# LayerNorm statistics from accumulated sums, and a sync queue that keeps program order for longer

## The chip, the cores and the metric

The kernel runs on one core of one Trainium2 chip, in one launch. The metric is the device time in microseconds (us), lower is better. Beside the time of a run there is one profiled execution, whose trace gives every instruction, its engine, its start and duration, and what ended the wait before it. The engines are PE (matrix multiply, with PEld for its weight loads), DVE (vector), ACT (activation), POOL (GpSimd) and SP, the sync queue, which issues all of this kernel's transfers.

## The reference, cut to what matters

Two residual blocks follow each other on 2048 tokens of width 640: attention with 32 heads over a sliding window of 256, and a gated MLP whose gate mixes tokens. All is fp32.

```python
h  = x + attention(layernorm(x), wqkv) @ wo
n  = layernorm(h)                              # over the 640 columns, eps 1e-5
z  = gelu(n @ w_in)                            # 1728 columns
z1, z2 = z[:, :864], layernorm(z[:, 864:])     # over 864 columns
g  = w_sp @ z2 + b_sp[:, None]                 # w_sp is 2048 x 2048: tokens by tokens
h2 = h + (z1 * g) @ w_out
```

## The kernel before, in words

Tokens go in 16 tiles of 128. Every fp32 product is made of three reduced-precision products: an operand is split in a high part (a copy on ACT) and a low part (raw minus high, on DVE). Many products also use Strassen's scheme, seven block products for eight, whose sums of blocks are DVE work. After attention the kernel goes through these stages:

- **Output projection and first LayerNorm** (loop over `i`, lines 1450 to 1488). In turn `i` PE multiplies tile `i` with `wo` (`proj_o`, 30 matmuls of 320 columns into one of two PSUM accumulators, `acc_tile`), DVE adds the residual to the tile before it (`add_h`, line 1438), and DVE and POOL make its statistics (`bn_h`): two `bn_stats`, one `bn_aggr` and one small addition on DVE (lines 1444, 90, 91), a power and a product on POOL (lines 92, 93). ACT then normalises (`scale_h`, line 97), PE transposes tile `i - 3` (`turn_h`, 5 transposes, line 932), ACT copies the transpose out and SP stores it to `hn_d`. DVE and ACT meanwhile scale and split later attention tiles (`norm_o` line 181, `split_o` lines 189 and 190) and prepare the first half of `w_in` (line 809 and 815, tiles `wraw`, `zl`). SP loads the attention output (`m`), the residual input (`xh`, 5 buffers) and `w_in`.
- **z1** (`z_pair`, steps 0 to 63): eight pairs of tiles, eight steps each; matmuls in line 992, into banks that ACT and DVE empty (lines 815, 809).
- **z2, first half** (`z2_pair` 8 to 11, steps 64 to 79): 15 matmuls a step (line 1050), a gelu out of PSUM on ACT (line 1055), LayerNorm statistics by `bn_stats` (line 1073), normalisation (line 97), and `right_blocks`, which makes the Strassen pieces `ze` and `zl`.
- **First gate** (`first_gate`, steps 80 to 135): eight pairs of seven steps, 12 matmuls a step (line 1160), for the first half of the token sum; the left pieces come from `w_sp` (`fx<-wsp_in`, line 1112), the result goes to `g_d` (lines 1199, 1200).
- **z2, second half** (`z2_pair` 12 to 15, steps 136 to 151) with inputs in buffers of its own (`z_r`, `z_a`), then the **second gate** (steps 152 to 207) and the **output product** (`out_pair`, steps 208 to 263).

Steps run in number order; `at(n, f)` places preparations, loads and stores ahead of step `n`. What order the instructions then stand in is set twice. Inside `manual_schedule` an engine keeps the order in which the code records. Outside it a scheduler orders each engine's instructions by its own timing estimate, and it may put instructions recorded outside a manual stretch ahead of ones recorded inside it. Before, the four engines PE, DVE, ACT and SP are manual from the start to step 62 and again from three steps into the second gate (step 155) to step 201, where the second gate's last pair begins; `ms.close()` and `in_order()` at the end of the code set this. On the chip each engine, SP too, takes its instructions strictly in the order so fixed.

## Time and profile before

| what | value |
|---|---|
| runs | 1110.23, 1115.27, 1112.72 us; median 1112.72 |
| the profiled execution's own time | 1112.77 us |
| its span, first to last instruction | 1111.1 us |
| busy shares of the span | PE 97%, PEld 88%, DVE 72%, ACT 53%, POOL 29% |
| mean granted PE clock | 0.997 |

The profiled execution's own time is 1.7 us over its span and within 0.1 us of the median. A busy PE in this trace need not be a PE at its full pace, as matmuls overlap: the number of matmuls in a stretch says more than its busy time, so the windows view is read with its counts.

### The profile page before, as it was taken

To read this page: it belongs to the slowest core of one execution; us is meant where nothing else is said; L and a number is where in the kernel's file an instruction comes from. 1 tells how busy PE (TensorE), PEld (TensorE's weight loads), DVE (VectorE), ACT (ScalarE), POOL (GpSimd) and SP (SyncE) were. 2 spreads that over 40 slices of the span, in tenths; PEclk is the share of its full clock that TensorE was granted. 3 is DMA by queue.
4 is the path that set the end of the run, shared out by engine and by line. 5 is a ranking of instruction groups with operands and counts; after the bars stand their busy time and mean duration, and the time that the engine had idled before them with its cause. 6 is when DMAs were issued, how large, how long until landed. Compare 5 with 4: busy or idle time off the path is not lost.

```text
span 1111.1 us, 28813 instructions
## 1 busy us (share of the span) xinstructions
PE 1078.4 (97%) x11083; PEld 973.7 (88%) x11083; DVE 804.5 (72%) x2185; ACT 584.8 (53%) x1202; POOL 318.3 (29%) x447
## 2 busy tenths in 40 slices
PE   8999999999999999999999999999999999999998
PEld 8998887668878787689889999999999899998998
DVE  6643444789999898687877678665448899987784
ACT  4443443259988898735565657443336533333331
POOL 4324446777766666723200002000001000000000
PEclk9999999999999999999999999999999999999999
DMA  7833557545565555689565531233431366674542
GB/s 250 295 114 118 175 182 266 174 159 190 187 188 187 175 181 159 186 248 307 210 226 179 200 117 58 78 106 116 140 123 42 119 236 239 242 270 142 192 142 95
DMA packets 92282, 194.74 MB, mean 175 GB/s; under 512 B 11952, under 2 KB 46272, under 8 KB 88256
## 3 DMA queue, kind: packets, MB, share of 16 engines
q1 hardware_dynamic: 92144, 192.90, 53.0%
q8 instruction: 87, 1.43, 0.5%
q14 instruction: 51, 0.42, 0.1%
HBM read 127.90 MB, written 64.95 MB: 174 GB/s over the span
## 4 chain that ended last, share of the span: by engine, by line
PE 47%; DMA 5%; DVE 4%; ACT 2%; issue 1%; SPq 1%; POOL 0%; DVEq 0%; ACTq 0%; POOLq 0%
PE g L1160 23%; PE zb L1050 9%; PE out_x L1324 3%; PE zx L992 2%; PE out_v L1324 2%; PE zv L992 2%; PE zy L992 1%; DMA m<-o_d 1%; PE out_y L1324 1%; PE wo_ps L106 1%; PE zw L992 1%; DMA xh<-x_in 1%; PE yt L1279 1%; DMA y_d<-row 1%; DVE m L181 1%
## 5 line engine op out<-in xcount | busy, mean ns | idle before, releaser
L402 ACT ACTIVATE pt<-bank 128x384 f32<-128x384 f32 (+1 forms) x452 | 179.2, 483 | 21.0 <-PE bank L399 13.4
L1160 PE MATMUL g<-zl,aw 128*128 128x432 f32 x768 | 168.7, 357 | 0.0
L356 DVE CUSTOM_DVE_ANT_0 junk<-bank,strip 128x288 bf16<-128x288 f32 x392 | 157.2, 453 | 13.3 <-PE bank L346 9.3
L815 ACT ACTIVATE aw<-fx 128x512 fp32r<-128x512 f32 (+2 forms) x152 | 86.3, 587 | 135.9 <-PE g L1160 60.6
L1160 PEld LDWEIGHTS g<-zl,aw 128*128 128x128 f32 x768 | 144.0, 188 | 6.2 <-DVE zl L809 0.3
L427 PE MATMUL pv<-pt,v_sb 128*32 128x192 f32 (+3 forms) x1984 | 136.1, 322 | 5.1 <-issue 2.3
L1160 PE MATMUL g<-ze,aw 128*128 128x432 f32 x576 | 132.4, 359 | 1.8 <-DVE row L809 1.7
L809 DVE TENSOR_TENSOR aw<-fx,aw 128x512 fp32r<-128x512 f32 (+2 forms) x152 | 95.8, 638 | 36.0 <-ACT aw L815 35.7
L1160 PEld LDWEIGHTS g<-ze,aw 128*128 128x128 f32 x576 | 107.1, 188 | 8.3 <-DVE row L809 2.6
L406 POOL TENSOR_SCALAR_AFFINE_SELECT pt<-pt 128x512 f32<-128x512 f32 x128 | 82.1, 641 | 56.7 <-ACT pt L402 51.5
L346 PE MATMUL bank<-slot 120*32 120x288 bf16 (+5 forms) x1280 | 95.1, 274 | 3.1 <-issue 1.5
L399 PE MATMUL bank<-slot 123*32 123x288 bf16 (+6 forms) x1296 | 96.3, 273 | 0.9 <-ACT pt L402 0.9
L92 POOL TENSOR_TENSOR mvz<-mvz,half 128x1 f32<-128x1 f32 x16 | 9.7, 606 | 301.5 <-DVE mvz L91 299.4
L427 PEld LDWEIGHTS pv<-pt,v_sb 128*32 128x32 f32 x1984 | 64.2, 110 | 12.4 <-POOL pt L406 5.3
L409 POOL TENSOR_SCALAR_AFFINE_SELECT pt<-pt 128x512 f32<-128x512 f32 x112 | 73.2, 653 | 0.0
L399 PEld LDWEIGHTS <-slot 123*32 123x32 bf16 x1728 | 61.7, 96 | 12.5 <-issue 3.0
L809 DVE TENSOR_TENSOR row<-g,row 128x432 f32<-128x432 f32 x80 | 48.3, 604 | 22.2 <-PE g L1160 21.9
L346 PEld LDWEIGHTS <-slot 120*32 120x32 bf16 x1440 | 51.9, 95 | 13.2 <-issue 6.6
L356 DVE CUSTOM_DVE_ANT_0 junk<-bank,mask 128x384 bf16<-128x384 f32 (+2 forms) x120 | 51.0, 447 | 16.7 <-PE bank L350 15.6
L603 POOL TENSOR_TENSOR sg<-rest,sg 128x512 bf16<-128x512 f32 x40 | 46.7, 1168 | 56.9 <-ACT sg L602 46.3
L593 DVE TENSOR_TENSOR rest<-qk,std 128x512 f32<-128x512 f32 x40 | 27.6, 690 | 47.7 <-PE qk L581 47.7
L106 PE MATMUL wo_ps<-xb,xb 128*128 128x320 f32 x260 | 53.5, 316 | 1.0 <-DVE xh L1438 1.0
(254 smaller groups left out, 2552.4 us busy)
## 6 DMA issues: line engine op xcount, KB each, us to landing
slot<-qk_d SPq DMA_DIRECT2D x144, 160.0 KB
fx<-wsp_in SPq DMA_DIRECT2D x32, 512.0 KB
qk_d<-sg SPq DMA_DIRECT2D x40, 384.0 KB
o_d<-ot SPq DMA_DIRECT2D x64, 128.0 KB
xb<-qk_d SPq DMA_DIRECT2D x48, 160.0 KB
fx<-hn_d SPq DMA_DIRECT2D x24, 320.0 KB
z_d<-row SPq DMA_DIRECT2D x16, 432.0 KB
g_d<-row SPq DMA_DIRECT2D x16, 432.0 KB
```

What stands on the lines that cost most here:

```text
L346: nc.tensor.matmul(ps[32 * j:32 * j + 32, o:o + w], one(st, 120, 0, hh, q0, 32), k, start=True, stop=True, tile_position=(0, 32 * j))
L356: nc.vector.tensor_tensor_reduce(out=junk[:, :n], in0=ps[:, :n], in1=keep, scale=1.0, scalar=NEG, op0=OP.add, op1=OP.max, accum_out=m_cols ...
L399: nc.tensor.matmul(ps[32 * i:32 * i + 32, b + o:b + o + w], one(st, 123, 1, hh, k0, 32), q, start=True, stop=True, tile_position=(0, 32 * i))
L402: nc.scalar.activation(pt[:, hh, :n], ps[:, :n], AF.Exp, scale=SCALE)
L406: nc.gpsimd.affine_select(out=pt[:, :, :P], in_=pt[:, :, :P], pattern=[[0, 4], [1, P]], base=0, channel_multiplier=-1, compare_op=OP.is_ge ...
L409: nc.gpsimd.affine_select(out=pt[:, :, 256:], in_=pt[:, :, 256:], pattern=[[0, 4], [-1, P]], base=-1, channel_multiplier=1, compare_op=OP. ...
L427: nc.tensor.matmul(ps[32 * hh:32 * hh + 32, a - 512 * c:b - 512 * c], v_sb[:, kb, v0:v0 + 32], pt[:, hh, a - kb * P:b - kb * P], start=fir ...
L809: (eng or nc.vector).tensor_tensor(out=out, in0=a, in1=b, op=op)
L815: nc.scalar.activation(out, a, AF.Copy)
L992: nc.tensor.matmul(ps, a[x], b[:, y], start=start and m + x + y == 0, stop=stop and m == n - 1 and x == 1, skip_group_check=True)
L1050: nc.tensor.matmul(b[0][:, :HF], a[:, x, kk], win2[0][:, y, kk, h * HF:(h + 1) * HF], start=kk + x + y == 0, stop=kk == KD - 1 and x == 1)
L1160: nc.tensor.matmul(ps, w[m][:, x, k], zc[k][m][:, y], start=start and k + x + y == 0, stop=stop and k == 3 and x == 1, skip_group_check=True)
```

## The change

It has two parts.

**Statistics.** For the first LayerNorm the residual addition becomes a DVE instruction that also accumulates the row sum (`tensor_tensor_reduce`, followed by an instruction that reads the accumulator). From the sum DVE makes the shifted bias (`squares_of`), ACT squares the tile around the mean with an accumulated sum, into a scratch tile `sq`, and DVE and POOL make the factors (`factors_of`). `scale_h` moves from the end of its turn into the next one. For pairs 12 to 14 of z2 the two gelus of a tile accumulate the row sums on ACT and the same helpers replace `bn_stats`; pairs 8 to 11 and 15 keep `bn_stats`. The residual input has 6 buffers instead of 5.

**Queue order.** SP alone keeps program order from the start to step 201 without a break, so also in z2, the first gate and the second gate's first three steps.

```diff
+    def squares_of(mv, junk, src, n, total, other=None):
+        nc.vector.tensor_scalar(out=mv[:, 1:2], in0=total, scalar1=0.0 if other is None else other,
+                                scalar2=-n ** -1.5, op0=OP.add, op1=OP.mult)
+        nc.scalar.activation(junk, src, AF.Square, bias=mv[:, 1:2], scale=n ** -0.5, accum_out=mv[:, 2:3])
+
+    def factors_of(mv, n):
+        nc.vector.tensor_scalar(out=mv[:, 3:4], in0=mv[:, 2:3], scalar1=EPS, scalar2=None, op0=OP.add)
+        nc.gpsimd.tensor_tensor(out=mv[:, 3:4], in0=mv[:, 3:4], in1=half, op=OP.pow)
+        nc.gpsimd.tensor_scalar(out=mv[:, 2:3], in0=mv[:, 1:2], scalar1=mv[:, 3:4], scalar2=n ** 0.5,
+                                op0=OP.mult, op1=OP.mult)
...
-    ms = ctx.enter_context(ExitStack())
+    sync_order, ms = (ctx.enter_context(ExitStack()) for _ in range(2))
+    sync_order.enter_context(tc.manual_schedule(engines={mybir.EngineType.SP}))
...
-            mybir.EngineType.PE, mybir.EngineType.DVE, mybir.EngineType.Activation, mybir.EngineType.SP}))
+            mybir.EngineType.PE, mybir.EngineType.DVE, mybir.EngineType.Activation}))
...
+        summed = 11 < q < 15
...
+                nc.scalar.activation(z[t][:, h * HF:(h + 1) * HF], b.pop()[:, :HF], AF.Gelu_apprx_tanh,
+                                     **({"accum_out": stats[t][0][:, h, 0:1]} if summed else {}))
...
+            if summed:
+                if h:
+                    squares_of(mv, win2[1][2], z[t], FH, st[:, 0, 0:1], st[:, 1, 0:1])
+                    factors_of(mv, FH)
+                return
...
     def add_h(i):
-        nc.vector.tensor_tensor(out=h3, in0=pre_ps.pop(0)[:, :, :HD], in1=h3, op=OP.add)
+        nc.vector.tensor_tensor_reduce(out=h3, in0=pre_ps.pop(0)[:, :, :HD], in1=h3, scale=1.0, scalar=0.0,
+                                       op0=OP.add, op1=OP.add, accum_out=stat_h[i][:, 0:1])
...
     def bn_h(i):
-        st, mv = stat_h[i] = stat_tiles(f"c{i}")
-        for j in range(2):
-            nc.vector.bn_stats(out=st[:, j, :], in_=hs[i][:, j * HD:(j + 1) * HD])
-        stats_of(mv, st)
+        mv = stat_h[i]
+        squares_of(mv, mem["sq"], hs[i], D, mv[:, 0:1])
...
+        if i > 1:
+            scale_h(i - 2)
         bn_h(i - 1)
...
+        factors_of(stat_h[i - 1], D)
         if i < NT:
             run(i - NT)
...
-        if i < NT:
-            scale_h(i - 1)
...
+        if n == e_start[1] + 49:
+            sync_order.close()
```

Three places show what moves. Line numbers are each kernel's own, so the same code has another number in the change. First DVE in one turn of the output projection, before: the addition, the statistics, then the low part of a later tile (`xb`), its scaling (`m`) and a piece of `w_in` (`zl`).

```order
L1438 TENSOR_TENSOR xh_9427<-wo_ps_10285,xh_9427 128x640
L1444 BN_STATS stc_10379<-xh_9427 128x6 x2
L90 BN_AGGR mvc_10380<-stc_10379 128x2
L91 TENSOR_SCALAR mvc_10380<-mvc_10380 128x1
L190 TENSOR_TENSOR xb_96<-m_9419,xb_95 128x640
L181 TENSOR_TENSOR m_9419<-m_9419,rs_9423 128x5x128
L146 TENSOR_TENSOR zl_10084<-wlast,zl_10084 128x432
```

The same turn in the change; the row `L1460 ISA` that writes 128x640 is the addition with its sum, the next reads the accumulator, `L103` is the step that needs ACT's squares.

```order
L1460 ISA xh_9434,mvc_10369<-wo_ps_10280,xh_9434 128x640
L1460 ISA mvc_10369 128x1
L98 TENSOR_SCALAR mvc_10369<-mvc_10369 128x1
L203 TENSOR_TENSOR xb_98<-m_9421,xb_97 128x640
L194 TENSOR_TENSOR m_9421<-m_9421,rs_9425 128x5x128
L103 TENSOR_SCALAR mvc_10369<-mvc_10369 128x1
L159 TENSOR_TENSOR zl_10088<-wlast,zl_10088 128x432
```

Three rows of statistics over the tile (two `BN_STATS`, one `BN_AGGR`) have gone, an accumulator read and a second small step have come, and the small step before `zl` now stands behind two long ones.

Second the sync queue early in z1, before: `z_r` is the input of z2's second half, `fx` that of the next z1 pair, `z_d` the store of a finished z1 tile.

```order
L1023 DMA z_d<-row_10087 128x864
L965 DMA fx<-hn_d 128x640
L1060 DMA z_r<-hn_d 128x640
L966 DMA fx<-hn_d 128x640
L883 DMA fx<-w_in_in 128x864
L1060 DMA z_r<-hn_d 128x640 x3
L1022 DMA z_d<-row_10088 128x864
L1060 DMA z_r<-hn_d 128x640
```

The same place in the change.

```order
L1037 DMA z_d<-row_10091 128x864
L979 DMA fx<-hn_d 128x640
L980 DMA fx<-hn_d 128x640
L896 DMA fx<-w_in_in 128x864
L1036 DMA z_d<-row_10092 128x864
L1037 DMA z_d<-row_10093 128x864
L979 DMA fx<-hn_d 128x640
```

The six `z_r` loads that stood in z1 have left it; all eight now stand among the last stores of the first gate. On ACT three copies `z_a<-z_r` (line 815) leave z1 with them.

Third the sync queue in the first gate, before: loads of `w_sp` (two for each pair) and stores of `g` by turns.

```order
L1112 DMA fx<-wsp_in 128x1024
L1200 DMA g_d<-row_10087 128x864
L1112 DMA fx<-wsp_in 128x1024
L1199 DMA g_d<-row_10088 128x864
L1112 DMA fx<-wsp_in 128x1024
L1200 DMA g_d<-row_10089 128x864
L1112 DMA fx<-wsp_in 128x1024
L1199 DMA g_d<-row_10086 128x864
```

The same place in the change.

```order
L1133 DMA fx<-wsp_in 128x1024 x2
L1220 DMA g_d<-row_10092 128x864
L1221 DMA g_d<-row_10093 128x864
L1133 DMA fx<-wsp_in 128x1024 x2
L1220 DMA g_d<-row_10090 128x864
L1221 DMA g_d<-row_10091 128x864
```

Both loads of a pair now stand together, ahead of both stores of the pair two before it.

## The prediction

> **What bounds the kernel now.** I read the page first, then windows by stage, then PE's waits and timeline in the stages that lose time.

> ```profile
> span 1111.1 us, 28813 instructions
> PE 1078.4 (97%) x11083; PEld 973.7 (88%) x11083; DVE 804.5 (72%) x2185; ACT 584.8 (53%) x1202; POOL 318.3 (29%) x447
> ```

> PE is the bound, so the change can only be worth time that PE loses. Its busy share hides some of that, so I count matmuls in windows (x is the count, then PEclk, DMA share, GB/s).

> ```profile
> core 0: us, PE busy (x) PEld busy (x) DVE busy (x) ACT busy (x) POOL busy (x), PEclk, DMA share, GB/s
> 483.25:551.83 68.58, 62.57 (x422) 61.02 (x420) 57.58 (x116) 35.10 (x55) 21.70 (x28) 0.98 0.83 272
> 500.00:524.00 24.00, 22.84 (x162) 22.61 (x161) 18.36 (x37) 12.63 (x20) 6.83 (x9) 1.00 1.01 315
> 524.00:552.00 28.00, 25.42 (x166) 24.76 (x165) 23.23 (x49) 14.38 (x23) 8.38 (x12) 0.94 0.62 224
> 542.20:545.50 3.30, 3.30 (x14) 3.30 (x13) 3.16 (x7) 1.51 (x2) 1.17 (x2) 0.50 0.23 89
> 570.00:600.00 30.00, 27.66 (x132) 25.66 (x132) 22.05 (x44) 17.15 (x33) 0.00 (x0) 0.94 0.67 235
> 583.20:586.50 3.30, 3.30 (x10) 3.00 (x10) 1.26 (x3) 1.48 (x3) 0.00 (x0) 0.50 1.01 370
> 600.00:640.00 40.00, 40.00 (x205) 38.03 (x204) 28.65 (x56) 25.79 (x50) 0.00 (x0) 1.00 0.54 186
> 692.00:870.00 178.00, 177.87 (x907) 169.55 (x906) 109.30 (x195) 81.37 (x147) 6.92 (x16) 1.00 0.29 96
> 870.00:890.00 20.00, 18.32 (x91) 16.40 (x90) 15.73 (x31) 8.33 (x15) 1.06 (x2) 1.00 0.50 169
> 890.00:980.00 90.00, 90.00 (x462) 86.31 (x461) 84.61 (x152) 29.82 (x57) 0.00 (x0) 1.00 0.68 239
> ```

> At full pace PE does 462 / 90 = 5.13 matmuls of 432 columns per us, and 205 / 40 = 5.13 in z1's later part. At 570 to 600 it does 132 where 154 fit: 22 / 5.13 = 4.3 us lost. From 692 to 870 it is short of 7 of 914, 1.3 us. At the start of the second gate, 870 to 890, it is short of 12, 2.3 us. In the output projection the transposes (L932) mark the turns.

> ```profile
> 483.25 0.71 PE L932 MATMUL ht_ps<-ident,hn 128*128 128x128 f32 x5
> 506.05 0.71 PE L932 MATMUL ht_ps<-ident,hn 128*128 128x128 f32 x5
> 511.00 0.71 PE L932 MATMUL ht_ps<-ident,hn 128*128 128x128 f32 x5
> 520.89 0.71 PE L932 MATMUL ht_ps<-ident,hn 128*128 128x128 f32 x5
> 540.88 0.53 PE L106 MATMUL wo_ps<-xb 128*128 128x320 f32 x2 [1.85 <-DVE xh L1438]
> 551.83 1.25 PE L932 MATMUL ht_ps<-ident,hn 128*128 128x128 f32 x10
> ```

> An undisturbed turn is 511.00 - 506.05 = 4.95 us. From 483.25 to 520.89 there are 7 turns in 37.6 us where 34.65 would do: 3.0 lost. From there to 551.83, 5 turns in 30.9 against 24.75: 6.2 lost. PE names its releaser:

> ```profile
> PE wo_ps L106 <- DVE xh L1438: 5.0, 6, 1.9
> ```

> With two accumulators, PE cannot start tile `i` until DVE has added tile `i - 2`. DVE is busy 23.2 of the last 28 us.

> **The change part by part.** *Statistics, output projection.* Prices:

> ```profile
> L1444 DVE BATCH_NORM_STATS2 stc<-xh 128x6 f32<-128x320 f32 x32 | 14.2, 485 | 0.5
> L90 DVE BATCH_NORM_AGGREGATE mvc<-stc 128x2 f32<-128x12 f32 x16 | 3.3, 209 | 1.4
> L91 DVE TENSOR_SCALAR mvc<-mvc 128x1 f32<-128x1 f32 x16 | 2.5, 154 | 0.7 <-DVE mvc L90 0.2
> L356 DVE DVE_READ_ACCUMULATOR2_ANT mcol<- 128x1 f32 x512 | 42.2, 82 | 0.0
> L1438 DVE TENSOR_TENSOR xh<-wo_ps,xh 128x640 f32<-128x640 f32 x16 | 13.0, 812 | 2.8 <-PE wo_ps L106 2.7
> L97 ACT ACTIVATE hn<-xh,mvc 128x640 f32<-128x640 f32 x16 | 14.7, 916 | 14.9 <-POOL mvc L93 14.9
> L189 ACT ACTIVATE xb<-m 128x640 fp32r<-128x640 f32 x12 | 8.7, 726 | 6.1 <-DMA r_d<-inv 6.1
> ```

> A tile sheds (14.2 + 3.3) / 16 = 1.09 us of DVE and gains an accumulator read (0.08) and one more small step (0.15): 0.86 less, 13.7 us over 16 tiles. The accumulating addition is not in the trace; between 0.81 (the plain one) and twice that I take 0.81, since its kin at L356 reads its accumulator in 0.08 with no idle time. At twice, the gain is spent. ACT gains a square for each tile, between 0.73 (L189, no operand in a tile) and 0.92 (L97, two); I take 0.9, or 14 us. ACT was busy 35.1 of 68.6 us, 2.9 per turn; 3.8 still fits in 4.95.

> The added waits: DVE's L103 step waits for ACT's square, and queued behind it are the `w_in` pieces and the next addition, for which PE waits. ACT's square waits for DVE's L98 step; behind it stand the `w_in` copies and the copy of the transposes. L103 stands behind two long DVE steps (L190 and L181 of before) of about 0.8 us each, as the next row shows one, and the square ends 0.9 us after L98, or 0.73 + 0.92 + 0.9 = 2.6 if the split and the normalisation ahead of it on ACT have not started: at most about 1 us of wait, which DVE can pay as its turn is 0.86 lighter and PE has one turn of slack. The normalisation moved by a turn no longer waits in its own turn for POOL; the transposes that read it come a turn later still.

> So a turn should come back to PE's 4.95 us. What else can hold it is transfers:

> ```profile
> 519.89 0.82 DVE L181 TENSOR_TENSOR m<-m,rs 128x640 f32<-128x640 f32 x1 [3.85 <-DMA xh<-x_in]
> ```

> Up to 524 the 16 DMA engines are full (share 1.01, 315 GB/s), and that 3.85 us wait is one for a load. An earlier PE only waits longer there. I give back 1 of the 3.0 us lost before 520.89, and 5 of the 6.2 after, where the DMA share is 0.62. Sum: 6.0; ends 0 (twice-priced addition, or DMA) and 9.2.

> *Queue order, z1.* Six `z_r` loads and their three ACT copies go.

> ```profile
> 570.37 4.78 SPq L1060 DMA_DIRECT2D z_r<-hn_d  x3
> 573.21 0.74 ACT L815 ACTIVATE z_a<-z_r 128x640 fp32r<-128x640 f32 x1 [1.98 <-issue]
> 577.73 1.36 ACT L815 ACTIVATE z_a<-z_r 128x640 fp32r<-128x640 f32 x2
> 581.91 1.57 PE L992 MATMUL zx<-zl,aw 128*128 128x432 f32 x6 [1.95 <-ACT row L815]
> 583.28 3.41 PE L992 MATMUL zv<-zl,aw 128*128 128x432 f32 x9
> ```

> ACT idles 1.98 us ahead of the first copy and spends 2.1 us on the three; PE then waits 1.95 us for ACT, and right behind it 3.3 us run at half clock (0.50 in the window above; 3.41 us for nine matmuls). Later pairs, without these copies, run at full pace. I take 4.0 of the 4.3 us; ends 2.0 (the wait alone) and 4.3.

> [...]

> *Queue order, z2 and gates.* PE loses only 1.3 us from 692 to 870, so program order can gain little. In the first gate both loads of a pair are issued five steps ahead of use, 5 x 12 / 5.13 = 11.7 us. In before one pair's loads took this:

> ```profile
> 729.99 0.33 SPq L1112 DMA_DIRECT2D fx<-wsp_in  x1
> ...
> 731.58 0.42 SPq L1112 DMA_DIRECT2D fx<-wsp_in  x1
> ```

> ```profile
> 737.88 0.63 ACT L815 ACTIVATE aw<-fx 128x512 fp32r<-128x512 f32 x1 [2.89 <-DMA fx<-wsp_in]
> ```

> That is 7.9 us from first issue to use, so 3.8 are spare. The first pair's `w_sp`, early in before, comes only in z2 and crowds DVE there: 0.5 us lost (ends -1.3 and 3). The eight `z_r` loads move into the end of the first gate, where a load has six steps, 14 us, before its use: nothing.

> *Statistics, z2.* For six tiles DVE sheds 12 `bn_stats` and 6 aggregations; ACT gains six squares of 864 columns.

> ```profile
> L1073 DVE BATCH_NORM_STATS2 stz<-row 128x6 f32<-128x432 f32 x32 | 19.2, 603 | 5.4 <-ACT row L1055 5.4
> L97 ACT ACTIVATE row<-row,mvz 128x864 f32<-128x864 f32 x16 | 17.7, 1105 | 6.5 <-POOL mvz L93 6.5
> ```

> DVE: 12 x 0.60 + 6 x 0.21 - 6 x 0.15 = 7.6 us less; ACT 6 x 1.1 = 6.6 more, with room, as PE runs full there. The 2.3 us at the second gate's start hang on tile pair 15, which is unchanged: 0.5 gained (ends 2.3 and -2).

> Sum against the profiled execution, 1112.8 us: 6.0 + 4.0 - 0.5 + 0.5 = 10.0, so **1102.8 us**. It agrees with the median of the runs to 0.1.

> **The rivals.** *DMA holds the output projection* (17%): for it, the share of 1.01 and the 3.85 us wait; against, the lost time is mostly after 524, at 0.62. It gives 1 instead of 6: 1107.8.

> *The half clock stays* (8%): if the two stretches of 3.3 us at half clock are due to something else than the waits, 2 x 1.65 = 3.3 us stay: 1106.1. For it, neither wait is as long as the stretch that follows; against, both stretches begin right behind PE's two longest waits. [...]

> *The accumulating forms save nothing* (5%): an addition at twice its price gives 1108.8 (6.0 lost).

> *The sync queue blocks the first gate* (12%, slower): one store of `g` that waits at the head of the queue holds the loads behind it.

> ```profile
> SPq L1199 <- DVE row L809: 70.9, 8, 15.2
> ```

> Such a store waited up to 15.2 us in before. If it holds a pair's loads beyond the 3.8 spare us, each of 8 pairs can lose a step, 12 / 5.13 = 2.3 us: 18.7 in all, 1102.8 + 18.7 = 1121.5. Against it: the loads now stand ahead of the stores of the same steps, where in before they stood behind them.

> **How the numbers follow.** The forecast itself has 58%. A measurement here tells about 0.5%, 5.6 us, from no change. Faster by more (under 1107.2): the forecast 58, the clock rival's 8, a part of the DMA rival, 4: 0.70. Slower: the queue rival 0.12. Within 0.5%: 0.18. Best end: 9.2 + 4.3 + 1.3 + 2.3 = 17.1, 1095.7; I cut the range at 1096.5. The upper end takes in the DMA and saving-nothing rivals, with 2 to 3 us of the gate's unknowns: 1111.5. Outside stay the queue rival and some tail, 2 in 10.

> **What would show it.** Right: turns of about 4.95 us between transposes throughout, no PE wait over 1.5 us for the addition, no half clock before 600, 154 matmuls in 30 us of early z1, and DVE about 14 us lighter in the projection. Wrong: DVE waiting for ACT's square for over 1 us a turn; loads of `m` or `xh` behind DVE's waits after 524; PE waiting on `aw` in the first gate, or a clock of 0.5 where no wait is.

## The result, and the profile after

The change makes the kernel faster by 0.7%: 1105.07 us (median of 6 runs, 1101.56 to 1106.83) against 1112.33 us (6 runs, 1110.23 to 1115.27), a ratio of 0.9932 with a 95% interval of 0.9911 to 0.9952. That is 7.3 us by the medians where 10.0 were forecast. The profiled execution after took 1106.83 us, the longest of its six.

The page after, first the span, then the engines: DVE is 22.9 us lighter, ACT 19.3 us heavier.

```profile
span 1105.1 us, 28802 instructions
PE 1075.1 (97%) x11083; PEld 970.4 (88%) x11083; DVE 781.6 (71%) x2157; ACT 604.1 (55%) x1258; POOL 314.3 (28%) x447
```

From the first matmul or transpose of each stage to that of the next, in the two profiled executions (a turn is counted from one tile's transposes to the next tile's):

| stage | before, us | after, us | gained | forecast |
|---|---|---|---|---|
| up to the twelve turns (attention) | 483.25 | 485.01 | -1.8 | 0 |
| twelve turns of the output projection | 68.58 | 62.79 | 5.8 | 6.0 |
| z1 | 90.98 | 87.83 | 3.2 | 4.0 |
| z2, first gate, z2 | 226.84 | 227.52 | -0.7 | -0.5 |
| second gate to its last matmul | 141.33 | 142.41 | -1.1 | 0.5 |
| from there to the end | 99.06 | 98.55 | 0.5 | 0 |

The first row is no work of the change: its instructions are the same, and in the 14 traces of this case it ends between 479.8 and 485.3 us. The two profiled executions differ by 5.9 us; without that row it would be 7.7, beside 7.3 by the medians.

The windows that answer to those of before (us, then PE, PEld, DVE, ACT, POOL busy with counts, PEclk, DMA share, GB/s); each is moved by as much as its stage:

```profile
485.01:547.79 62.78, 60.17 (x422) 59.41 (x420) 45.42 (x104) 45.29 (x82) 16.76 (x28) 1.00 0.88 294
485.01:521.28 36.27, 34.91 (x248) 34.65 (x246) 25.50 (x57) 24.81 (x45) 8.65 (x15) 1.00 0.97 311
521.28:547.79 26.51, 25.25 (x177) 24.76 (x175) 19.92 (x48) 20.48 (x37) 8.11 (x14) 1.00 0.77 271
566.00:596.00 30.00, 29.61 (x151) 28.06 (x151) 22.25 (x45) 17.71 (x34) 0.00 (x0) 1.00 0.55 190
684.80:862.80 178.00, 177.25 (x904) 168.95 (x903) 105.51 (x187) 90.66 (x174) 6.50 (x14) 1.00 0.30 99
863.30:883.30 20.00, 17.73 (x87) 15.68 (x86) 16.83 (x31) 9.26 (x16) 2.04 (x4) 1.00 0.65 219
```

The same 422 matmuls and transposes stand in 62.8 us where they took 68.6, with DVE at 45.4 us where it had 57.6. Early z1 does 151 matmuls in 30 us where it did 132, and no clock is under 1.00. The second gate's start does 87 in 20 us where it did 91. What is left in the projection are three waits of PE, in the first, eighth and eleventh turn (6.57, 5.74 and 5.93 us; the other nine take 4.94 to 4.97):

```profile
487.07 0.56 PE L118 MATMUL wo_ps<-xb,xb 128*128 128x320 f32 x2 [1.35 <-DVE mvc L1460]
522.52 0.56 PE L118 MATMUL wo_ps<-xb 128*128 128x320 f32 x2 [0.54 <-DVE mvc L1460]
538.34 0.56 PE L118 MATMUL wo_ps<-xb 128*128 128x320 f32 x2 [0.72 <-DVE mvc L1460]
```

The prices that before could not show, as groups (count | busy us, mean ns | idle before):

```profile
L1460 DVE CUSTOM_DVE_ANT_0 xh<-wo_ps,xh 128x640 f32<-128x640 f32 x16 | 13.0, 812 | 3.3 <-PE wo_ps L118 3.3
L1460 DVE DVE_READ_ACCUMULATOR2_ANT mvc<- 128x1 f32 x16 | 1.3, 84 | 0.0
L103 DVE TENSOR_SCALAR mvc<-mvc 128x1 f32<-128x1 f32 x16 | 2.4, 152 | 6.5 <-ACT sq L100 6.1
L100 ACT ACTIVATE sq<-xh,mvc 128x640 f32<-128x640 f32 x16 | 13.1, 817 | 0.0
L100 ACT ACTIVATION_READ_ACCUMULATOR sq<-xh,mvc 128x1 f32 x16 | 3.0, 188 | 0.0
L1073 ACT ACTIVATION_READ_ACCUMULATOR row<-zb 128x1 f32 x12 | 2.3, 192 | 0.0
```

The accumulating addition costs what the plain one did (0.81 us); its sum is 0.08 us more. A square with its sum is 0.82 + 0.19 = 1.0 us of ACT.

### The profile page after: what moved, and what is told of

The parts are those of the page before. It is cut to its first block, busy times and chain, and to the rows that moved or that the text cites. A ratio compares the mean times of both kernels' runs of the same rounds, so it can differ in the third digit from the quotient of the medians.

```text
span 1105.1 us, 28802 instructions
## 1 busy us (share of the span) xinstructions
PE 1075.1 (97%) x11083; PEld 970.4 (88%) x11083; DVE 781.6 (71%) x2157; ACT 604.1 (55%) x1258; POOL 314.3 (28%) x447
## 4 chain that ended last, share of the span: by engine, by line
PE 43%; DMA 4%; issue 4%; ACT 3%; DVE 3%; POOL 2%; SPq 0%; ACTq 0%; POOLq 0%; DVEq 0%
PE g L1181 23%; PE zb L1066 4%; PE out_x L1345 3%; PE zx L1006 2%; PE out_v L1345 2%; PE zv L1006 2%; DMA h_d<-xh 1%; PE zy L1006 1%; PE zw L1006 1%; PE out_y L1345 1%; PE yt L1300 1%; DMA fx<-wsp_in 1%; DVE row L822 1%; PE wo_ps L118 1%; ACT pt L417 1%
## 5 line engine op out<-in xcount | busy, mean ns | idle before, releaser
L369 DVE CUSTOM_DVE_ANT_0 junk<-bank,strip 128x288 bf16<-128x288 f32 x392 | 157.1, 452 | 14.9 <-PE bank L359 12.9
L608 ACT ACTIVATE sg<-rest 128x512 bf16<-128x512 f32 x40 | 25.2, 631 | 53.5 <-DVE rest L606 53.5
```

The source lines that it names most:

```text
L369: nc.vector.tensor_tensor_reduce(out=junk[:, :n], in0=ps[:, :n], in1=keep, scale=1.0, scalar=NEG, op0=OP.add, op1=OP.max, accum_out=m_cols ...
```

## The experiments

My theory after the result was the prediction's: the statistics pay in the projection, because DVE is lighter; the queue order pays in z1 and costs a little in the gates; the stretches at half clock come from PE's waits. The rivals were that the moved normalisation did it, that the queue order served the projection, and that the half clock was chance. Each ratio is against the kernel before on the same chip; stage times are from the run's profile, as in the table above.

| run | ratio, 95% interval | twelve turns | z1 | z2, gate, z2 | second gate |
|---|---|---|---|---|---|
| the change | 0.9932, 0.9911 to 0.9952 | 62.79 | 87.83 | 227.52 | 142.41 |
| statistics of the projection alone | 0.9947, 0.9920 to 0.9975 | 62.91 | 90.18 | 226.83 | 141.65 |
| queue order alone | 0.9994, 0.9973 to 1.0016 | 66.57 | 87.18 | 228.10 | 142.29 |
| move and sixth buffer alone | 0.9970, 0.9950 to 0.9989 | 65.29 | 91.23 | 226.87 | 141.55 |
| projection's sums without the move | 0.9994, 0.9973 to 1.0016 | 70.86 | 90.88 | 226.85 | 141.33 |
| change, z2 with `bn_stats` | 0.9956, 0.9930 to 0.9981 | 64.33 | 87.88 | 227.64 | 142.22 |
| change, queue order to z1's end only | 0.9953, 0.9936 to 0.9969 | 63.61 | 92.34 | 226.83 | 142.33 |
| change, epsilon on POOL | 0.9934, 0.9910 to 0.9957 | 62.33 | 87.86 | 232.22 | 142.16 |
| change, a second pass before each square | 1.0006, 0.9989 to 1.0023 | 66.85 | 88.83 | 228.05 | 142.08 |
| change, `rs` loads first | 0.9971, 0.9954 to 0.9989 | 65.67 | 87.87 | 232.59 | 142.72 |
| change, early gate loads | 0.9951, 0.9932 to 0.9970 | 65.34 | 87.84 | 227.42 | 142.07 |
| the same and spread `w_in` pieces | 0.9935, 0.9913 to 0.9957 | 61.60 | 87.84 | 227.22 | 142.11 |
| change, graded waits in z1 (one run) | none | 64.84 | 99.78 | 228.84 | 142.41 |

**The projection's statistics alone.** The change, with the queue part taken out and z2 left with `bn_stats`.

```diff
-    sync_order.enter_context(tc.manual_schedule(engines={mybir.EngineType.SP}))
...
-        summed = 11 < q < 15
+        summed = False
```

> The first LayerNorm alone: accumulated sums and squares, the moved normalisation and the sixth buffer; z2 and the sync queue are as before the change. Theory (the parts add up, each in its own stage): the twelve turns of the output projection take about 62.8 us as after the whole change (68.6 before), z1 keeps its 91.0 us with the stall behind the z_r copies, and the kernel takes about 1112.3 - 5.8 = 1106.5 us. Rival (the queue order is what freed the projection, since loads of m, rs and xh come in time by it): the turns stay near 68 us, 1112.

The turns take 62.91 us and z1 keeps its stall (90.18): 5.9 us of the 7.3 by the ratio are this part's (2.8 to 8.9 by its interval), and the turns show no share of the queue order. One profile is a rough measure of the turns, though: the six runs with the change's own projection code took 62.79 to 65.34 us, the two with that of before 66.57 and 68.58.

**The queue order alone.** Before, with SP manual from the start to step 201.

```diff
+    sync_order.enter_context(tc.manual_schedule(engines={mybir.EngineType.SP}))
...
+        if n == e_start[1] + 49:
+            sync_order.close()
```

> The sync queue's order alone, statistics as before. Theory (the parts add up): z1 shrinks from 91.0 to about 87.8 us as after the whole change, the turns stay near 68 us, the second gate's side loses about 1, and the kernel takes about 1112.3 - 2.5 = 1109.8 us. Rival (queue order also serves the projection): turns near 65 us or less and 1107. Rival (z1 gained only since the clock stayed up, by chance): z1 stays above 89 us.

z1 shrinks to 87.18 us as expected, but the time stays within the interval of no change (0.9994): z2 to z2 costs 1.3 us more than before and the second gate 1.0. Alone, the order lies between 3 us faster and 2 slower, so that its gain in z1 is seen in the stage and its net worth is not shown.

**Move against sums.** Two kernels complete a square of four for the projection: the move and the sixth buffer with `bn_stats`, and the sums with the normalisation left at the end of its own turn.

```diff
+        if i > 1:
+            scale_h(i - 2)
         bn_h(i - 1)
...
-        if i < NT:
-            scale_h(i - 1)
```

> Before the change, with only the normalisation moved into the next turn and the sixth buffer; bn_stats stay, the queue is as before. Theory (DVE's load is what the projection gained by, about 0.86 us for a tile): the turns stay within 1.5 us of 68.6 and the kernel within 1.5 us of 1112.3. Rival (the order did it: ACT no longer waits for POOL within a turn, so its copies and splits come earlier): turns of about 64 us and 1107.

The second takes these same lines out of the kernel with the projection's statistics alone. Both have the sixth buffer; no run has the buffer by itself.

> The accumulated sums in the output projection without the moved normalisation: it stands at the end of its own turn, as before the change; six buffers, queue and z2 as before. With the run that only moved it, and the one that has both, this makes a square of four. Theory (the two add up): moving alone gave 1.7 us of turns outside the half-clock stretch, both gave 4.1, so the sums alone give about 2.4: turns of about 64.7 us and 1109. Rival (the sums need the move, since ACT's normalisation waits for POOL behind the square and holds up the copies): turns no shorter than 67, 1111 or more.

Neither theory held, and the second run came out as its rival said. The move with the buffer is worth 3.3 us by its ratio (1.2 to 5.6); the sums without the move lie between 3 us faster and 2 slower; both together are worth 5.9. That the sums need the move is shown, as the intervals of the two kernels with sums just meet (0.9973 to 1.0016, and 0.9920 to 0.9975). That the move needs the sums is not: 0.9950 to 0.9989 overlaps with 0.9920 to 0.9975, so the 2.6 us between them are not clear of noise. The turns take 65.3 us with the move, 70.9 with the sums and 62.9 with both; the 65.3 lie at the upper end of the spread of the change's own code (62.79 to 65.34). Of before's 68.6, 1.5 are a stretch at half clock (shown below), and the 70.9 hold two. Waits of ACT and DVE in the turns (total us, times, longest) show why the sums alone are lost. Before, for ACT and for DVE:

```profile
ACT hn L97 <- POOL mvc L93: 14.9, 8, 2.4
```

```profile
DVE xb L190 <- ACT xb L189: 1.9, 4, 0.6
```

With the sums and without the move, ACT and then DVE, and one such wait:

```profile
ACT hn L108 <- POOL mvc L104: 14.0, 9, 2.4
```

```profile
DVE xb L202 <- ACT xb L201: 17.1, 11, 2.3
```

```profile
504.68 0.83 DVE L202 TENSOR_TENSOR xb<-m,xb 128x640 fp32r<-128x640 f32 x1 [2.05 <-ACT xb L201]
```

After the change, the same two:

```profile
ACT hn L109 <- POOL mvc L105: 2.0, 4, 0.9
```

```profile
DVE xb L203 <- ACT xb L202: 4.4, 4, 2.2
```

Left in its turn, the normalisation holds ACT for 14 us waiting for POOL's factors; the copy that starts a split (`xb`) stands behind it, and DVE, in order, waits 17.1 us for that copy. ACT waited as long before (14.9), but DVE, busy for 57.6 us of the turns with its statistics, reached the copy late and waited 1.9 for it; with the sums it is busy for 45.0. What DVE sheds in statistics it then spends standing. Moved by a turn, ACT waits 2.0 us. What the move alone gains by is less clear. In its profile PE's waits in the turns fall from 6.0 to 4.4 us and no stretch there runs at half clock; DVE's wait for the copy could give it only the 1.9 us.

**How much room the square has.** A second, unused pass of ACT ahead of each square.

```diff
         mv = stat_h[i]
+        nc.scalar.activation(mem["sq"], hs[i], AF.Square)
```

> After the change, with a second, unused pass of ACT over each of the 16 tiles just ahead of the square (about 0.72 us each, 11.5 in all), so that DVE's step behind the square waits longer; it adds work and leaves none out. Theory (ACT has room, and one turn of slack covers DVE's wait): the twelve turns grow by at most 3 us, from 62.8 to under 66. Rival (ACT or the wait behind the square already sets the turn): each added pass shows in full, 12 x 0.7 = 8.5 us, turns of about 71 us, 1113.

The turns grow by 4.1 us, between the two. DVE's waits at the step behind the square go from 4.3 to 13.3 us, of which 5.8 reach PE in five waits, against 2.6 in three:

```profile
DVE mvc L103 <- ACT sq L100: 13.3, 12, 2.2
```

```profile
PE wo_ps L118 <- DVE mvc L1460: 5.8, 5, 1.9
```

So the wait for the square is not free: twelve passes of 0.73 us, 8.7 in all, cost PE 4.1, about half. By the ratios the kernel loses 8 us; z1 takes another 1.0 of them, and the rest I did not place.

**Taking that wait off DVE.** The addition of epsilon goes to POOL.

```diff
-        nc.vector.tensor_scalar(out=mv[:, 3:4], in0=mv[:, 2:3], scalar1=EPS, scalar2=None, op0=OP.add)
+        nc.gpsimd.tensor_scalar(out=mv[:, 3:4], in0=mv[:, 2:3], scalar1=EPS, scalar2=None, op0=OP.add)
```

> After the change, with the small addition of epsilon (the step of DVE that waits for ACT's square) put on POOL, for the projection and for z2's six tiles. Theory (what is left of the lost time in the turns is DVE standing in front of ACT's square): the first and last long turns, 6.57 and 5.93 us after the change, fall towards 5.2, the twelve turns from 62.8 to about 61 us, and the kernel to about 1103.5. Rival (the copies and additions behind that step wait for something else anyway): turns as after the change, 62.8, and 1105.

The first turn is clean (4.95 us), but the second and third take 5.49 and 5.98, the eleventh 6.10: 62.33 us in all and the same ratio. The wait moved; the rival holds.

**What paces the eighth turn.** The loads of `rs` go ahead of those of `m`.

```diff
-            load_o(i // 2 + 3)
             load_sums(i // 2 + 3)
+            load_o(i // 2 + 3)
```

> After the change, with the load of rs put ahead of the four loads of m instead of behind them, at each of the output projection's places where the two are issued. Theory (the eighth turn is paced by transfers, and the last of them is the rs load, issued at 513.1 us and used at 519.7): rs comes some 4 us earlier, DVE's wait of 3.9 us there shrinks by at least 1.5, the eighth turn goes from 5.74 us to about 5, and the kernel takes about 1104.3 us. Rival (the transfer engines are full there, so whichever load is last lands at the same time): DVE waits as long, for m or xh in place of rs, the eighth turn is 5.7 us or more, 1105.

DVE waits as long, as the rival has it. First DVE's wait in the eighth turn after the change, then in this run with PE's wait that follows, then the same two in the run with early gate loads, whose projection has the change's own code:

```profile
519.67 0.82 DVE L194 TENSOR_TENSOR m<-m,rs 128x640 f32<-128x640 f32 x1 [3.92 <-DMA rs<-r_d]
```

```profile
521.82 0.83 DVE L194 TENSOR_TENSOR m<-m,rs 128x640 f32<-128x640 f32 x1 [5.09 <-DMA xh<-x_in]
...
524.67 0.90 PE L118 MATMUL wo_ps<-xb 128*128 128x320 f32 x2 [3.04 <-DVE mvc L1460]
```

```profile
519.42 0.83 DVE L194 TENSOR_TENSOR m<-m,rs 128x640 f32<-128x640 f32 x1 [3.80 <-DMA rs<-r_d]
...
522.26 0.76 PE L118 MATMUL wo_ps<-xb 128*128 128x320 f32 x2 [3.35 <-DVE mvc L1460]
```

`rs` was issued 3.4 us earlier and DVE waited longer, for `xh`; the turn took 9.71 us. The last kernel began the turns 2.3 us earlier than the profiled execution after the change (482.74 against 485.01), and PE went on at nearly the same moment, 522.26 against 522.52: there an earlier PE only waited longer (10.09 us for that turn). Both long turns also hold a stretch at half clock behind the wait, by an estimate from 3.41 us at 0.50 some 1.7 us of each. First with `rs` ahead, then with the early gate loads:

```profile
524.51:527.92 3.41, 3.25 (x12) 3.25 (x13) 2.40 (x7) 3.41 (x7) 0.35 (x1) 0.50 0.87 190
```

```profile
522.45:525.86 3.41, 3.41 (x14) 3.41 (x14) 2.49 (x5) 3.41 (x7) 0.69 (x1) 0.50 1.06 171
```

In the 14 traces the eighth turn takes 4.95 to 10.09 us, and DVE stands 2 to 5 us for a load on the way to it in each; in one of them, the run with spread `w_in` pieces, none of that reaches PE. With `rs` ahead the kernel is slower than the change (0.9954 to 0.9989 against 0.9911 to 0.9952), where the rival said the same time. Its profiled execution, 1115.05 us, is the longest of twelve and also loses 5.1 us in z2 and the first gate, so one profile does not show where the others lose.

**The losses in z2 and the gates.** Three runs. The queue's order ended at z1's end:

```diff
-        if n == e_start[1] + 49:
+        if n == 62:
             sync_order.close()
...
-            in_order()
+            in_order(mybir.EngineType.SP)
```

> After the change, but the sync queue keeps program order only up to z1's end; from there it is as before the change. Theory (the order pays in z1 and costs in the gates): z1 stays at about 87.8 us, the 0.7 us lost at the first gate's start and the 0.6 at the second gate's come back, and the kernel takes about 1103.7 us. Rival (those losses belong to the sums in z2, which stay): the gates lose as after the change, 1105.

z1 was worse than before, 92.34 us: the `z_r` loads are recorded after step 62, and outside the order they are put ahead again. The queue, an ACT pair and PE in z1 of this run:

```profile
566.01 5.48 SPq L1079 DMA_DIRECT2D z_r<-hn_d  x3
...
574.07 1.35 ACT L828 ACTIVATE z_a<-z_r 128x640 fp32r<-128x640 f32 x2
...
578.25 1.44 PE L1006 MATMUL zx<-zl,aw 128*128 128x432 f32 x6 [2.64 <-ACT row L828]
```

After the change the first of them is issued at 806.48 us, and PE's waits on `zx` in z1 are 0.9 us in three (2.6 before). That shows the `z_r` loads to be z1's stall. The loss of 0.7 us in the first gate went, as expected of the order; the second gate's did not.

z2 with `bn_stats`:

```diff
-        summed = 11 < q < 15
+        summed = False
```

> After the change, but z2 keeps bn_stats for all its tiles. Theory (PE runs full there, so neither engine's load counts): within 1 us of the whole change, 1105, with z2 and the gates as long as there. Rival (the sums in z2 cost at the second gate's start, by ACT's six squares and twelve accumulator reads): about 1 us faster than the whole change, with the 0.7 us lost between the first gate and the end of z2 given back.

Within 0.12 us in z2 and 0.2 in the second gate: the theory holds there, the sums in z2 are worth nothing. (Its turns took 1.5 us more than the change's, with the same code.) At the second gate's start PE waits 1.7 us before and 2.3 after the change,

```profile
PE g L1160 <- DVE row L809: 1.7, 2, 1.0
```

```profile
PE g L1181 <- DVE row L822: 2.3, 4, 0.7
```

and 2.3 with the order but `bn_stats`, 2.3 with the sums but no order there, 1.7 with neither: either part alone costs the 0.6 us, and they do not add up.

The first pair's loads of the gate issued at step 58 instead of 69:

```diff
-        at(e0 - 11 if p != 1 else n0 - 10, load)
+        at(n0 - 10 if p == 1 else e0 - (22 if p == 0 and c == 0 else 11), load)
```

> After the change, with the first gate's first pair of w_sp loads issued at step 58 instead of 69, so that program order no longer keeps them back into z2. Theory (the 0.7 us wait at the first gate's start comes from these late loads and the copies that they push together): that wait goes, the stretch from z2's first part to the end of its second, 227.3 us after the change, falls by 0.7 to the 226.6 of before, and the kernel takes about 1104.4 us. Rival (the wait comes of other steps that the order changed): it stays at 0.7 to 1.0 us.

PE's wait in the first gate after the change, and in this run at z2's beginning:

```profile
690.87 0.47 PE L1181 MATMUL g<-zl,aw 128*128 128x432 f32 x1 [0.70 <-ACT zl L828]
```

```profile
638.35 0.87 PE L1066 MATMUL zb<-win,aw 128*128 128x432 f32 x3 [0.48 <-ACT row L828]
```

The 0.70 us went, as the theory said, and 0.48 came elsewhere: 227.42 us, no gain. With one more `w_in` piece in each of two turns as well:

```diff
-        if i in (4, 6):
+        if i in (4, 6, 8, 10):
```

> After the change, with the early gate loads of the run beside it and one more piece of w_in in each of the turns 8 and 10 of the output projection, where DVE stands waiting for loads, so that fewer are left for the turn of 5.93 us, in which DVE has five pieces ahead of the addition. Theory (that turn is long because DVE's pieces stand ahead of the addition): it falls towards 5.2 us, the twelve turns from 62.8 to about 62.1, and the kernel to about 1103.7. Rival (the pieces only move the wait, since their w_in loads come late in a stage whose transfers are full): turns of 62.8 or more, 1104.4 or more.

The eighth and eleventh turns were clean in its profile, 4.95 and 4.94 us, the ninth took 6.10; the twelve took 61.60 us. That is nearer to the theory than to the rival, but this profiled execution, 1099.79 us, is the shortest of its six, and its turns began at 479.76, earlier than in any other trace. Its ratio, 0.9935, is the change's own: no better version is shown.

**The half clock.** Unused ACT passes of about 1 us (after the change a square over the same 128x864 elements takes 1.01) ahead of the seventh step's additions, two in pair 1 of z1 and one more in each later pair.

```diff
+            for _ in range(q + 1 if 0 < q else 0):
+                nc.scalar.activation(win2[1][2], zl[q].rearrange("p a b -> p (a b)").bitcast(F32), AF.Square)
             plus(c22, ps("x"), tmp1[:, :HF])
```

> After the change, with two to eight unused passes of ACT over 128x864 elements (about 1 us each) put ahead of the seventh step's additions in z1's pairs 1 to 7, two in pair 1 and one more in each pair, so that PE waits for ACT, longer in each pair; it adds work and leaves none out. Theory (a half-clock stretch follows where waits leave PE busy for little over half of one of the 3.413 us windows on which the stretches lie): the pairs with waits under 1.6 us bring no stretch; those with 2 us and more bring one each when the wait falls in one window, and every window of z1 in which PE is busy for 0.52 or less is followed by one at 0.50, no window at 0.53 or more. Rival (the stretches are not due to the waits): none or one in z1, wherever it falls. [...]

PE's four longest waits in z1 of this run:

```profile
599.78 1.45 PE L1006 MATMUL zx<-zl,aw 128*128 128x432 f32 x6 [0.88 <-ACT row L828]
613.05 1.46 PE L1006 MATMUL zx<-zl,aw 128*128 128x432 f32 x6 [2.21 <-ACT row L828]
628.17 2.47 PE L1006 MATMUL zx<-zl,aw 128*128 128x432 f32 x6 [2.71 <-ACT row L828]
642.46 0.67 PE L1006 MATMUL zw<-zl,aw 128*128 128x432 f32 x2 [1.89 <-ACT aw L828]
```

And the windows that hold the last three, each of the first two with the one behind it:

```profile
611.20:614.61 3.41, 1.55 (x8) 1.49 (x9) 2.68 (x6) 1.80 (x5) 0.00 (x0) 1.00 0.99 289
614.61:618.02 3.41, 3.41 (x11) 3.18 (x10) 2.32 (x5) 2.10 (x4) 0.00 (x0) 0.50 0.60 239
...
624.85:628.26 3.41, 0.70 (x5) 0.33 (x3) 1.68 (x5) 3.27 (x8) 0.00 (x0) 1.00 0.73 183
628.26:631.68 3.42, 3.42 (x10) 3.19 (x11) 2.43 (x6) 1.41 (x3) 0.00 (x0) 0.50 0.79 301
638.50:641.91 3.41, 2.07 (x11) 1.64 (x9) 1.23 (x3) 3.41 (x7) 0.00 (x0) 1.00 0.21 80
```

The waits of 2.21 and 2.71 us fell mostly within one window each, leaving PE busy for 0.46 and 0.21 of it, and the next window ran at half clock. The 1.89 us wait was divided between two windows (0.61 in the first), and nothing followed. In this one run, waits made on purpose bring the half clock, so the rival that has it from something else falls. But not every one does: this same run has a window with 0.45 in the projection, at 519.04, without a sequel, and the queue-order run has a twin of before's. Before, and the same two windows in that run:

```profile
538.74:542.15 3.41, 1.56 (x12) 1.35 (x11) 3.24 (x9) 2.78 (x5) 0.00 (x0) 1.00 0.26 102
542.15:545.57 3.42, 3.42 (x15) 3.42 (x15) 3.28 (x8) 1.51 (x2) 1.17 (x2) 0.50 0.24 92
```

```profile
538.74:542.15 3.41, 1.56 (x13) 1.34 (x11) 3.38 (x7) 2.97 (x5) 0.00 (x0) 1.00 0.27 102
542.15:545.57 3.42, 3.42 (x24) 3.42 (x25) 3.28 (x8) 1.03 (x3) 1.18 (x2) 1.00 0.49 194
```

PE is busy for the same 1.56 us, with the same wait of 1.85 us in it; one goes on at half clock with 15 matmuls, the other at full clock with 24, and that turn takes 8.57 and 7.04 us. So my "every window of 0.52 or less" was too strict, and what decides between the two is open.

## Why the prediction was right, point by point

It said faster, and 1105.07 lies in its range, 2.3 us above the predicted time. Step by step:

- **The turn returns to 4.95 us.** Nearly: nine of twelve do, and the sum is 5.8 us against 6.0. The split holds too: the first seven turns gave 1.4 (37.64 to 36.27) against 1, the last five 4.4 (30.94 to 26.52) against 5. Of the 4.4, 1.5 is before's half clock, which the queue-order run lost by chance with the same code. And this pair of profiles is a lucky one: the spread of the turns with either projection (62.79 to 65.34, and 66.57 to 68.58) allows 1.2 to 5.8.
- **Why it does** was the step that failed. The prediction put the gain to DVE's 0.86 us a tile and gave the moved normalisation one sentence and no price. The square of four shows no gain by the sums alone (0.9994) and 3.3 us by the move, with its buffer; whether the 2.6 us beyond that are the sums' is open. The forecast sum came out right because the two stood in the same edit.
- **Prices.** The addition took the lower end, 0.81 us, as chosen. The square with its read is 1.0 us against 0.9. DVE lost 22.9 us against 13.7 + 7.6 = 21.3, ACT gained 19.3 against 14 + 6.6 = 20.6. The rival of accumulating forms that save nothing is out.
- **The wait behind the square, at most about 1 us.** Six waits, the longest 1.39 us, and that one reached PE as 1.35 us. The run with a second pass shows about half of such time to reach PE.
- **DMA holds the projection.** Not this rival as a whole, but its ground is real and can be larger than the 1 us that I left for it: DVE waits 2 to 5 us for a load ahead of the eighth turn in every trace, and in 13 of the 14 that turn is long, 5.18 to 10.09 us; this is part of what the runs of one kernel differ by.
- **z1, 4.0 us.** 3.2: waits on `zx` fell from 2.6 to 0.9 us, and a stretch at half clock went. The early window won 19 of its 22 matmuls, 3.7 us, and some 0.5 us was lost elsewhere in z1, for which I had no term. By one pair of profiles the stretch was priced too high at 1.65 us: without it, but with the loads, z1 took 90.18 us in the run with the projection's statistics alone, against 90.98. That the `z_r` loads are the cause is shown by the run that let them back, and in all traces but the graded one z1 took 87.2 to 88.8 us without them there and 90.2 to 92.3 with them.
- **The half clock comes from the waits.** Shown for waits of 2.2 and 2.7 us. Both are shorter than the 3.41 us stretches that followed them, so what the prediction put down for the rival, that neither wait in before was as long as its stretch, does not speak against the waits. The stretches' starts lie whole multiples of 3.4133 us apart, about a stretch's own length: 583.11 - 542.15 = 40.96 us in before is twelve times that, and 1104.82 - 241.25 = 863.57 us after the change 253 times. Windows on this grid in which PE was busy for 0.46 and 0.43 (before, from 538.74 and 579.70) were followed by a stretch.
- **First gate, 0.5 us.** 0.7, and it goes with the order: z2, gate and z2 took 226.83 to 226.87 us in every trace without it. The price is not a steady one, and 0.7 is its lower end: with the order and the gate's loads unmoved it was 0.7 to 2.0 us in five profiles, and 5.4 and 5.8 in two (epsilon on POOL, `rs` first) with 6.8 us at half clock. So z1's gain is in part given back here. The blocked queue, 18.7 us, did not come.
- **Second gate, gain of 0.5.** A loss of 0.6 at its start, and 1.1 over the stage. The prediction took tile pair 15 as unchanged and so left the start a small gain; either part alone costs there, by a way that no run shows.
- **Sums in z2.** Worth nothing, as forecast; PE is busy for 177.25 of the 178 us from 684.8 after the change, and for as good as all of them before (177.87), so neither DVE's load nor ACT's shows.

What stays open: how the 0.5 us over the start's 0.6 in the second gate come about, what the sums add to the move, why two like windows differ in what follows, and what makes the first gate's loss large in some profiles.

## What to carry to other kernels

An edit that changes both what an engine does and when it does it should be priced as two edits: here the lighter DVE showed no gain while ACT's normalisation stood in front of the copy that DVE needs next. Where a wait is on the last of several loads, work taken out ahead of it need not be gained: here turns that began 2.3 us earlier went on only 0.26 us earlier (522.26 with the early gate loads, at a DMA share of 0.99 in the window of the wait, against 522.52). Changing the loads' order changed which one was last, and cost time (a ratio of 0.9971 against 0.9932). Compare a stage over several profiles of the same code before reading a gain of 2 us from one pair. Keep a queue's program order past the place where the loads are recorded that must not come early, not only past the place where they hurt.
